# Declaring instructions on different banks of one PSUM pair free of each other

## The chip, the cores and the metric

The kernel runs on one core of a Trainium2 chip. A core has a matrix engine (TensorE, PE in the profile, its weight loads listed apart as PEld), three engines for element-wise work (VectorE, DVE; ScalarE, ACT; GpSimd, POOL) and queues that start transfers (DMA). Each engine works through its own list of instructions in the order in which they were written, and engines wait for each other through semaphores. The metric is the device time of one execution in microseconds (us).

PSUM is the memory into which PE writes. It has eight banks for each of its 128 partitions, each with 512 float32 values. This kernel uses all eight, as four pairs.

## The reference

Two layers follow each other. For 8 batches of 576 positions and 8 heads of width 64, the first is attention in a symmetric window of 32 positions. Its output, 512 numbers for a position, goes into the second: a router picks 2 of 4 experts for each position, each expert is a causal attention head of width 64 with an output projection, and the two picked outputs are added with the router's weights.

```python
scores = q @ k.T / 8                      # each batch and head
attn = softmax(where(abs(i - j) <= 32, scores, -1e9))
x = (attn @ v) as (batch, position, 512)
logits = x @ w_gate                       # (batch, position, 4)
w = softmax over the two largest logits
for e in range(4):
    a = softmax(causal((x @ wq[e]) @ (x @ wk[e]).T / 8))
    out += w[e] * (a @ (x @ wv[e]) @ wo[e])
```

## The kernel before

The whole work is cut into steps, and a text, `ORDER` (line 24), lists them in the order in which each engine is to meet them. There is no planner at run time: the loop at line 590 calls the function with the step's name, and the digits after the name are its arguments (batch, group of heads or pair of experts, tile). After `@` stand the PSUM banks that the step uses, and a letter names the engine of a copy: a for ACT, v for DVE, g for POOL. So `pt010@1` is the function `pt` for batch 0, expert pair 1, part 0, in bank 1, and `ot010@1a` is the copy of its result by ACT.

The steps of one batch, each with its engine:

- loads `lq`, `lk`, `lv` by the DMA queue of the sync engine. A load waits for the PE instruction that was written last before it (lines 175 to 179), so loads keep pace with PE;
- `tq`, `tk` (DVE) transpose q and k in blocks; `sc` (PE) makes the window's scores, `ex` (ACT) their exponentials, `mk` (POOL, at times DVE) the mask;
- `av` (PE) multiplies by v, `un` (DVE) divides by the sum, `xt` (PE) transposes the result, `xf` (ACT or DVE) copies it from PSUM, `xb` casts it to bfloat16;
- the gate: `ga` (PE) makes the logits, `gt` and `gm` (DVE, lines 442 to 456) transpose them and find the two largest, `ge` (ACT, line 448) takes exponentials, `gu` (DVE, lines 461 to 464) makes the weights. These five keep all that they need in one bank;
- the experts: `pp` and `pv` (PE) project, `pe` and `ve` copy the results out, `ps` (PE) makes scores, `xe` (ACT) exponentials, `se` (POOL) the causal mask, `po` (PE) multiplies by v, `oe` (DVE) divides and weighs, `pt` (PE) transposes, `ot` copies that out, `py` (PE) projects, `ye` copies to the tile Y, `st` stores.

Steps of several batches lie in each other's gaps in `ORDER`. All PE instructions are issued by `mm` (line 170) or `tr` (line 173), and all copies by `copy` (lines 152 to 158), so the profile shows these lines; which step it is follows from the tiles and the order.

What counts for this change is how PSUM is held. The four tiles `PS0` to `PS3` are pairs of banks:

```python
PS = [psum.tile([128, 2, 512], F32, name=f"PS{i}") for i in range(4)]
def two(bank):
    return PS[bank // 2]
def one(bank):
    return PS[bank // 2][:, bank % 2, :]
```

Banks 0 and 1 are `PS0`, 2 and 3 `PS1`, 4 and 5 `PS2`, 6 and 7 `PS3`. The wide steps (`sc`, `ex`, `av` and `un` of the first four tiles, `pp`, `pe`, `ps`, `xe`, `po`, `oe`) take a whole pair through `two`. The narrow ones take a single bank through `one`: the gate's five, `pt` and `ot`, and the last, shorter tile of `av`, `un`, `xt`, `xf`, `pv`, `ve`, `py` and `ye`. Two narrow steps can so stand in the two banks of one pair at the same time.

The framework in which the kernel is written draws the dependencies between instructions by itself, from the tiles that they write and read, and sets the waits on semaphores. In the kernel before, instructions of two engines on different banks of one pair do wait for each other in places: the trace shows PE on bank 1 released by DVE on bank 0.

Of the kernel before, what the change touches and what calls it, by code (L numbers as in the profile page):

```python
# [89 lines left out]
"""  # L90


@with_exitstack
def kernel(
    ctx: ExitStack,
# [8 lines left out]
    moe_wo: bass.AP,  # L104
    out: bass.AP,
):
    nc = tc.nc
    B, H, S_, D = q.shape
    E, DM, HD = moe_wq.shape
    assert S_ == S and D == 64 and H == 8 and HD == 64 and DM == 512 and E == 4  # L110
# [12 lines left out]
    PS = [psum.tile([128, 2, 512], F32, name=f"PS{i}") for i in range(4)]  # L123
# [19 lines left out]
    ident = sb.tile([128, 128], F32, name="ident")  # L143
# [51 lines left out]
        nc.scalar.activation(RC[1], RC[0], EXP)  # L195

    def s_ident():
        make_identity(nc, ident)
        nc.gpsimd.tensor_copy(ident_bf, ident)

    def s_ones():
# [386 lines left out]
    with tc.manual_schedule():  # L588
        nc.vector.memset(RC[0], 0.0)
        for step in ORDER.split():  # L590
            name, _, banks = step.partition("@")
# [35 lines left out]
```

The softmax here doesn't subtract the row's maximum and nothing guards it: scores larger than these inputs give would overflow.

## Time and profile before

| | |
|---|---|
| time, median of 3 runs | 263.46 us (263.01 to 265.67) |
| span of the profiled execution | 263.2 us |
| mean granted clock of PE | 0.978 |
| PE's share of the chain that ended last | 73% |
| DVE's, ACT's, DMA's share of it | 12%, 5%, 4% |
| read from and written to memory outside the core | 30.42 MB, 9.44 MB |

The chain that ended last is followed back from the last instruction: at each step to what released it, or to the instruction ahead of it on its engine. An engine's idle time matters only where this chain goes through it. In the timeline, a line is a run of like instructions: when it started, how long it took, engine, source line, operation, out<-in tiles, shape, count, and in brackets the idle time of the engine ahead of it with what ended it. A line "DVE L464" is the last instruction of `gu`, "PE L173 PS<-ident_bf,OE" is `pt`, "PE L170 PS<-WO,OTT" is `py`.

### The profile page before, as it was taken

Reading aid. Unit: us, or ns where it says so; the run is one execution under the profiler, and the core shown is the slowest. Engines: PE = TensorE matmul, PEld = TensorE weight load, DVE = VectorE, ACT = ScalarE, POOL = GpSimd, SP = SyncE. Lnnn points to the kernel's source line nnn. Section 1 sums busy time; section 2 is a strip of 40 time slices with the busy share of each in tenths; the row PEclk is TensorE's granted clock in tenths of the full one; section 3 lists DMA queues with packets and bytes.
Section 4 is the critical chain, followed back from the end, with each engine's and each line's share of the span. In section 5 each row is a group of like instructions: output and inputs, shape, how many; then the busy total and the mean of one; then the engine's idle time right before and its main releaser. Section 6 shows DMA issues by size and latency. Waiting matters only on the chain.

```text
span 263.2 us, 12340 instructions
## 1 busy us (share of the span) xinstructions
PE 217.3 (83%) x5523; PEld 173.8 (66%) x5536; DVE 186.4 (71%) x381; ACT 155.2 (59%) x236; POOL 149.0 (57%) x164
## 2 busy tenths in 40 slices
PE   0386988999997899889779699989799698998762
PEld 0375767877796588767567577867687476875440
DVE  7977868998889668768467778959655344467360
ACT  2057674886686476567626677637455675656333
POOL 5049778189949953489726932797535652311110
PEclk9999999999999799999999999999999799999798
DMA  7969578868888356598728533443302104040225
GB/s 244 283 174 268 120 158 269 224 192 208 215 243 212 122 139 204 165 241 214 244 65 232 170 112 95 125 133 75 110 22 85 72 11 182 2 158 5 101 93 189
DMA packets 55382, 40.65 MB, mean 154 GB/s; under 512 B 45345, under 2 KB 46369, under 8 KB 55329
## 3 DMA queue, kind: packets, MB, share of 16 engines
q1 hardware_dynamic: 54672, 38.62, 51.3%
q10 hardware_dynamic: 656, 1.25, 1.3%
q8 instruction: 43, 0.70, 1.0%
q14 instruction: 11, 0.08, 0.1%
HBM read 30.42 MB, written 9.44 MB: 151 GB/s over the span
## 4 chain that ended last, share of the span: by engine, by line
PE 73%; DVE 12%; issue 6%; ACT 5%; DMA 4%; SPq 0%; DVEq 0%; ACTq 0%
PE PS L170 65%; PE PS L173 8%; DVE XTB L158 2%; DMA kn<-in_k_dram 2%; DMA V<-in_v_dram 1%; ACT Y L154 1%; ACT A L346 1%; ACT ATE L516 1%; DVE Tkn L299 1%; DVE Tkn L287 1%; DVE Y L158 1%; DVE PS L442 1%; ACT OTT L154 1%; DVE OTT L158 1%; DVE XTF L158 0%
## 5 line engine op out<-in xcount | busy, mean ns | idle before, releaser
L350 POOL TENSOR_TENSOR A<-A,MASKP 128x576 f32<-128x576 f32 x62 | 87.2, 1428 | 43.2 <-ACT A L346 43.2
L516 ACT ACTIVATE ATE<-PS 128x1024 bf16<-128x1024 f32 (+1 forms) x64 | 51.0, 837 | 24.8 <-PE PS L170 23.5
L170 PE MATMUL PS<-Tqn,Tkn 32*64 32x128 f32 (+2 forms) x2560 | 46.4, 275 | 14.5 <-DVE Tqn L299 10.6
L346 ACT ACTIVATE A<-PS 128x576 f32<-128x576 f32 x64 | 38.6, 651 | 33.5 <-PE PS L170 30.4
L170 PEld LDWEIGHTS PS<-Tqn,Tkn 32*64 32x64 f32 x2560 | 40.9, 140 | 18.8 <-DVE Tqn L299 10.8
L523 POOL TENSOR_SCALAR_AFFINE_SELECT ATE<-ATE 128x512 bf16<-128x512 bf16 (+1 forms) x48 | 25.2, 539 | 42.9 <-ACT ATE L516 42.8
L170 PE MATMUL PS<-V,A 128*64 128x65 f32 (+1 forms) x1280 | 40.0, 222 | 7.3 <-issue 3.1
L170 PEld LDWEIGHTS PS<-V,A 128*64 128x64 f32 (+1 forms) x1280 | 36.3, 131 | 11.5 <-issue 4.8
L287 DVE STREAM_TRANSPOSE Tkn<-kn 128x576 f32<-128x576 f32 x28 | 32.6, 1242 | 3.2 <-PE PS L170 1.7
L287 DVE STREAM_TRANSPOSE Tqn<-qn 128x576 f32<-128x576 f32 x28 | 32.6, 1242 | 1.6 <-DMA qn<-in_q_dram 1.6
L170 PE MATMUL PS<-WO,OTT 128*128 128x512 bf16 (+1 forms) x83 | 19.6, 355 | 8.5 <-DVE G L464 2.5
L376 DVE TENSOR_TENSOR XN<-PS,RC 128x512 f32<-128x512 f32 x32 | 22.1, 692 | 1.2
L156 POOL COPY V<-V 64x1024 f32<-64x1024 f32 (+1 forms) x22 | 21.8, 993 | 1.8 <-POOL A L350 0.5
L154 ACT COPY XTF<-PS 128x1024 f32<-128x1024 f32 (+1 forms) x26 | 16.6, 676 | 8.0 <-PE PS L173 5.2
L170 PE MATMUL PS<-WV,XTB 128*128 128x256 bf16 (+1 forms) x192 | 20.0, 264 | 0.7 <-ACT ATE L516 0.4
L173 PE MATMUL PS<-ident,XN 128*128 128x128 f32 x144 | 19.7, 277 | 1.1 <-issue 0.8
L170 PE MATMUL PS<-XTB,WQ 128*128 128x288 bf16 x128 | 19.0, 296 | 1.5 <-DVE XTB L158 1.4
L154 ACT COPY Y<-PS 128x1024 f32<-128x1024 f32 (+1 forms) x18 | 15.0, 839 | 8.0 <-PE PS L170 7.4
L170 PE MATMUL PS<-XTB,WK 128*128 128x288 bf16 x128 | 19.6, 300 | 0.0
L156 POOL CAST XTB<-XTF 128x128 bf16<-128x128 f32 (+1 forms) x18 | 10.9, 622 | 13.3 <-ACT XTF L154 12.7
L170 PEld LDWEIGHTS <-ATE 128*128 128x128 bf16 x480 | 16.6, 97 | 2.5 <-issue 1.2
L173 PEld LDWEIGHTS PS<-ident,XN 128*128 128x128 f32 x144 | 15.6, 140 | 4.0 <-issue 2.7
(70 smaller groups left out, 271.8 us busy)
## 6 DMA issues: line engine op xcount, KB each, us to landing
V<-in_v_dram SPq DMA_DIRECT2D x32, 256.0 KB, 3.9
out_dram<-Y SPq DMA_DIRECT2D x16, 512.0 KB, 3.4
kn<-in_k_dram SPq DMA_DIRECT2D x14, 576.0 KB, 5.0
qn<-in_q_dram SPq DMA_DIRECT2D x14, 576.0 KB, 4.2
kn<-in_k_dram SPq DMA_DIRECT2D x4, 288.0 KB, 5.1
qn<-in_q_dram ACTq DMA_DIRECT2D x4, 288.0 KB, 5.5
V<-in_v_dram SPq DMA_DIRECT2D x8, 128.0 KB, 3.9
out_dram<-Y SPq DMA_DIRECT2D x15, 64.0 KB, 2.2
```

The source lines that it names most:

```text
L154: nc.scalar.copy(o, i)
L156: nc.gpsimd.tensor_copy(o, i)
L158: nc.vector.tensor_copy(o, i)
L170: PACE[0] = nc.tensor.matmul(*args, **kw)
L173: PACE[0] = nc.tensor.transpose(*args)
L287: nc.vector.transpose(T[:, dh, :].rearrange("q (p o) -> q o p", o=18), n_[:, :, 32 * dh:32 * dh + 32])
L299: nc.vector.transpose(QKT[nm][g][:, dh, :].rearrange("q (p o) -> q o p", o=18)[:, 9 * x:9 * x + 9, :], NAT[nm][g][:, 9 * x:9 * x + 9, 32 * ...
L346: nc.scalar.activation(a_part(b, g, half, p), two(b0)[:, :, 0:HS], EXP, scale=scale_att)
L350: (nc.gpsimd if eng == "g" else nc.vector).tensor_tensor(out=ap, in0=ap, in1=MASK[:, None, HS * half:HS * half + HS].to_broadcast([128, 2, ...
L376: nc.vector.tensor_tensor(out=XN[T // 2][:, T % 2, :].rearrange("p (g h d) -> p g h d", g=2, h=4), in0=u[:, :, :, 0:64], in1=rc[:, :, :, N ...
L516: nc.scalar.activation(A[:, at:at + 2 * step].rearrange("p (e x) -> p e x", e=2)[:, :, 0:w], two(b0)[:, :, 0:w], EXP, scale=scale_moe)
L523: nc.gpsimd.affine_select(ap, ap, pattern=[[0, n], [1, w]], compare_op=IS_GE, fill=0.0, base=64 * j if c == 3 else 0, channel_multiplier=-1)
```

## The change

The kernel's `nc` is wrapped. Each call on PE, DVE, ACT and POOL is issued as before, and then noted with the boxes that it reads and writes: tile, partitions and range; for a PSUM tile all partitions and whole banks. For each of the last 100 noted instructions of the same tile on another engine, if no two boxes overlap with at least one write, the wrapper declares that the two do not depend on each other. It is for the narrow steps above: two that stand in the two banks of one pair need not wait for each other any more. Instructions that start loads and stores are not noted. The step list, the instructions and their operands are the same.

```diff
--- before.py
+++ after.py
@@ -90,6 +90,62 @@
 """
 
 
+class Watched:
+
+
+
+    def __init__(self, tc):
+        self.tc, self.tiles = tc, {}
+        self.tensor, self.vector, self.scalar, self.gpsimd = (
+            Engine(self, e) for e in (tc.nc.tensor, tc.nc.vector, tc.nc.scalar, tc.nc.gpsimd))
+        self.sync = tc.nc.sync
+
+    @staticmethod
+    def boxes(i):
+        found = []
+        for aps, write in ((i.ins.ins, False), (i.ins.outs, True)):
+            for a in aps:
+                b = getattr(a, "bass_ap", None)
+                if b is None:
+                    continue
+                row, n = b.ap[0]
+                p0, lo = divmod(b.offset, row)
+                hi = lo + sum(st * (m - 1) for st, m in b.ap[1:]) + 1
+                if b.tensor.name.startswith("PS"):
+                    p0, n, lo, hi = 0, 128, 2 * lo // row, (2 * hi - 1) // row + 1
+                    row = 2
+                found.append((b.tensor.name, p0, p0 + n, lo / row, hi / row, write))
+        return found
+
+    @staticmethod
+    def clash(x, y):
+        return (x[0] == y[0] and (x[5] or y[5]) and x[1] < y[2] and y[1] < x[2] and x[3] < y[4] and y[3] < x[4])
+
+    def note(self, engine, i):
+        mine = self.boxes(i)
+        done = set()
+        for name in {x[0] for x in mine}:
+            seen = self.tiles.setdefault(name, [])
+            for e, theirs, j in seen:
+                if e is not engine and j.ins.name not in done:
+                    done.add(j.ins.name)
+                    if not any(self.clash(x, y) for x in mine for y in theirs):
+                        self.tc.declare_no_dep(i.ins, j.ins, reason="no common element")
+            self.tiles[name] = seen[-100:] + [(engine, mine, i)]
+        return i
+
+
+class Engine:
+    def __init__(self, watched, engine):
+        self._w, self._e = watched, engine
+
+    def __getattr__(self, name):
+        f = getattr(self._e, name)
+        if name == "dma_start":
+            return f
+        return lambda *a, **k: self._w.note(self._e, f(*a, **k))
+
+
 @with_exitstack
 def tile_sliding_window_symmetric__then__jetmoe_attn_experts_kernel(
     ctx: ExitStack,
@@ -104,7 +160,7 @@
     moe_wo: bass.AP,
     out: bass.AP,
 ):
-    nc = tc.nc
+    nc = Watched(tc)
     B, H, S_, D = q.shape
     E, DM, HD = moe_wq.shape
     assert S_ == S and D == 64 and H == 8 and HD == 64 and DM == 512 and E == 4
@@ -195,7 +251,7 @@
         nc.scalar.activation(RC[1], RC[0], EXP)
 
     def s_ident():
-        make_identity(nc, ident)
+        make_identity(tc.nc, ident)
         nc.gpsimd.tensor_copy(ident_bf, ident)
 
     def s_ones():
```

## Prediction

> **What bounds the kernel now.** I read the page first (its busy times, its clock row and the chain of waits that ended last), then the chain in order of time, then the timeline around each place where TensorE (PE) stood still, then windows over those places.
>
> ```profile
> span 263.2 us, 12340 instructions
> PE 217.3 (83%) x5523; PEld 173.8 (66%) x5536; DVE 186.4 (71%) x381; ACT 155.2 (59%) x236; POOL 149.0 (57%) x164
> PEclk9999999999999799999999999999999799999798
> PE 73%; DVE 12%; issue 6%; ACT 5%; DMA 4%; SPq 0%; DVEq 0%; ACTq 0%
> ```
>
> PE is busy for 83% of the span and is 73% of the chain; the rest of the chain is short visits to VectorE (DVE, 12%) and ScalarE (ACT, 5%). So the kernel is PE's work plus the stalls in PE's queue. Three digits of the clock row fall to 7, in slices of 6.6 us that begin near 86, 204 and 243 us (the 8 at the end is the tail). By windows, 0 to 84 us has 67.0 us of PE work and DMA engines busy for 0.80 of the time; 84 us to the end has 150.3 us of PE work in 179.2, so 28.9 us of PE idle, and DMA at 0.41. The question is how much of these 28.9 us is a wait between two banks of one pair. Three places in the timeline show the type:
>
> ```profile
> 84.14 0.10 PEld L173 LDWEIGHTS <-OE 128*128 128x128 bf16 x1
> 85.41 0.38 DVE L442 STREAM_TRANSPOSE PS<-PS 128x160 f32<-128x160 f32 x1
> 86.28 0.44 PE L173 MATMUL PS<-ident_bf,OE 128*128 128x128 bf16 x5 [2.07 <-DVE PS L445]
> ...
> 203.48 0.37 DVE L442 STREAM_TRANSPOSE PS<-PS 128x160 f32<-128x160 f32 x1 [2.08 <-PE PS L173]
> 205.18 1.02 PE L170 MATMUL PS<-WO,OTT 128*128 128x512 bf16 x3 [1.81 <-ACT A L346]
> 206.33 0.69 ACT L154 COPY OTT<-PS 128x640 bf16<-128x640 bf16 x1 [0.68 <-DVE G L464]
> 207.08 0.69 PE L173 MATMUL PS<-ident_bf,OE 128*128 128x128 bf16 x5 [0.88 <-ACT OTT L154]
> ...
> 245.00 0.64 PE L170 MATMUL PS<-WO,OTT 128*64 128x256 bf16 x4 [2.45 <-DVE G L464]
> ```
>
> The first is step pt010@1: five transposes into bank 1. They waited 2.07 us for the gate step gt2@0, which works in bank 0 of the same pair and which DVE could start only at 85.41, after other work. The third is py52@7, which waited 2.45 us for gate step gu7@6. Neither pair of steps shares an element: OE and OTT come from elsewhere, and the banks differ.
>
> ```profile
> 84.17:87.58 3.41, 1.34 (x17) 1.17 (x15) 2.09 (x6) 1.88 (x3) 3.35 (x4) 1.00 0.52 181
> 87.58:90.99 3.41, 3.19 (x12) 1.68 (x12) 2.90 (x10) 1.45 (x3) 3.41 (x4) 0.50 0.57 172
> 203.63:207.04 3.41, 0.97 (x3) 0.38 (x4) 2.04 (x11) 1.97 (x5) 1.83 (x2) 1.00 0.00 0
> 207.04:210.46 3.42, 3.38 (x18) 2.33 (x18) 0.67 (x1) 2.04 (x3) 2.29 (x2) 0.50 0.32 126
> 241.17:244.59 3.42, 1.38 (x33) 0.71 (x22) 2.21 (x11) 2.46 (x4) 1.47 (x3) 1.00 0.01 2
> 244.59:248.00 3.41, 3.00 (x16) 1.94 (x17) 0.32 (x2) 1.30 (x2) 0.64 (x1) 0.50 0.11 28
> ```
>
> These are windows over those places; after the length comes PE's busy time, and the number after the last bracket is the granted clock. Each time PE was busy for less than 1.4 us of 3.41, the next 3.41 us ran at half clock. So these stalls are paid twice.
>
> **What the Trainium skill says.** "PSUM — Partial Sum Buffer", section "PSUM bank collisions raise a hardware error", says that two engines on one bank and quadrant at once are an error, reads included, while the same pairs on different banks run clean. So a wait between two banks guards nothing; no trace here shows a collision. "TensorE: Matmul & The Clock Gate", section "What's actually happening", says that the clock is halved after an idle window of about 3.4 us of a free-running grid. The trace agrees on 3.41 us and on the half, but shows that a window with 0.97 to 1.38 us of work is idle enough. "Perfetto Trace Analysis", section "Identifying Dependency Chains", says that an instruction that waits for several engines may have extra wait instructions put ahead of it; PE's queue has 44 such semaphore instructions here, most of 0.05 us.
>
> **The change part by part.** No instruction is added or taken away and the step list is the same, so the busy times stay. The wrapper, whose host-side code costs the chip nothing, withdraws the dependency between two instructions of different engines unless they share a box: for PSUM a bank, for SBUF a range, with at least one write. Loads are not wrapped, so they keep their waits and their pacing. Pairs of reads of one bank (ACT and DVE) are freed too; PE refills the bank between them and both sides still wait for PE, so I put that at nothing. What is left is the sum over steps that sit alone in one bank of a pair. I list PE's idle time there from the timeline, and what I take after asking which true wait comes next.
>
> - pt010@1 behind gt2@0, 84.1: 2.07. The eight WQ matmuls behind it follow with no wait of their own. Take 2.0.
> - av34@3 behind ye02@2a, 106.0: 0.46. Take 0.45.
> - xf32@2a on ACT behind ot100@3v on DVE, 114.62. PE's gate matmuls truly wait for it, idle 0.84; ACT could have begun at 114.2 when PE's transposes ended. Take 0.4.
> - pt110@3 behind gu3@2, 119.4: 0.43 on the weight load, but the short matmul before overlaps. Take 0.3. py12@7 behind un44@6, 127.1: 0.27. Take 0.2.
> - pt200@1 behind gu4@0, 147.1: 2.75. Its successor pv30 needs the ACT step that ended at 144.7 and started at 147.35. Take 2.6.
> - ga5@1 behind ot300@0v, 175.2: 1.03. Take 1.0. Then gt5@1 on DVE waited for pt310@0 until 177.45, and behind it ACT's exponentials, for which PE idled 0.36 at 179.5. Take 0.3.
> - ve51@4a on ACT behind un64@5 on DVE: ACT starts at 186.85 in place of about 186.1, behind it the exponential for which PE idled 1.40 at 188.5. Take 0.7.
> - xt62@3 behind ye32@2v, 192.5: 0.26. Take 0.25.
> - gt6@6 on DVE behind pt410@7 on PE, 203.48: DVE idle 2.08. Behind gt6 ACT's ge6 waits, and behind ge6 the exponential for which PE idled 1.81. Then ot410@7a waited for gu6@6, and pt400@6 for ot410: another 0.88. Together 2.69. pt400@6 shares bank 6 with gu6, so that wait stays, but gu6 ends about 2 us sooner. Take 2.6.
> - av74@1 behind ot500@0a, 221.1: 1.15. Take 1.1.
> - py52@7 behind gu7@6, 245.0: 2.45. Take 2.4.
> - In the tail, ot711@3a on ACT behind ye62@2v on DVE: ACT runs at 255.14, though PE's transposes ended near 253.5; PE idles 1.61 for it. Take 1.4.
>
> The sum is 15.7 us. Halved clock: 3.41 us at half speed lose 1.7 us of work, three times: 5.1. The ceiling is 20.8 us.
>
> Two things take some back. Between these places ACT and DVE release PE's banks with little to spare (PE idles of 0.2 to 0.4 us for them are all along the timeline), so part of a freed microsecond meets the next true wait. And the clock's windows lie on a fixed grid, so another thin stretch (the tail, or the 2.35 us at 130 us in which PE waited for nothing that the profile shows, and which I leave as it is) may now fill one. The trace bounds neither; from 0 to all, I keep 70% of the stalls (11.0) and two of three half-clock spells (3.4): 14.4 us, so 263.46 - 14.4 = 249.1 us.
>
> **The rivals.**
> - Nearly all of it comes back: 263.5 - 20.8 = 242.7. For it: after 84 us DVE is busy for 113.9 of 179.2 us, ACT 103.8, POOL 93.2, so each has room to run earlier with PE. Against it: POOL is busy for 9.85 us of the 10 from 80 to 90.
> - The waits change their name. PE is released early and stops at the next ACT or DVE release. Half of the four large places (2.0, 2.6, 2.6, 2.4), none of the small ones and no clock: 4.8, so 258.7. For it: ACT and DVE hold 17% of the chain.
> - No change: DVE's and ACT's own queues set the pace, and only the tail's 1.4 remains: about 262. Against it: DVE and ACT were idle at these places or had work that nobody needed soon.
> - Slower. A wait that stood for several is gone, and the others appear on their own: some 30 more wait instructions in PE's queue at 0.05 make 1.5. Loads are paced by PE's progress, so a PE that runs ahead sends them into DMA engines already busy (0.62 to 0.66 from 90 to 152 us), and one late k load of 5.0 us to landing lies on the path in full: 263.5 + 1.5 + 5.0 - 3 (a fifth of the stalls) = 267. Against it: the only large DVE waits for loads are 1.6 and 1.5 us in the whole span.
>
> **How the numbers follow.** Main case 0.62, nearly all 0.12, renamed waits 0.14, no change 0.08, slower 0.04. So faster by over 1% (below 260.8) is 0.88, within 1% 0.08, slower 0.04. The range from 241.5 to 258.5 holds the main case with both ends of the take-back and the full case, and leaves out about half of the renamed case, the unchanged and the slower one.
>
> **What the profile after would show.** Right: the idle of 2.07, 2.75, 2.69 and 2.45 us at these steps gone, PE's busy time down by the clock share (about 3 of 217) and its share of the span up to 86% or more, DVE's and ACT's busy times unchanged, the digits 7 before the tail mostly gone. Wrong: equally long idle of PE in the same stretches under another releaser (ACT A, ACT ATE or DVE XTB), new half-clock windows elsewhere, or DVE waits for loads of several microseconds.

## The result, and the profile after

The changed kernel takes 241.92 us (median of 4 executions, 240.37 to 243.94). The kernel before, run beside it, took 263.47 us. The ratio is 0.9171, with a 95% interval from 0.9079 to 0.9264; here and below, a ratio leaves out the executions of a kernel that took over 1.5% longer than its fastest. The forecast was 249.1 us with a range from 241.5 to 258.5: right in direction and inside the range, but at its lower end. What happened is the rival "nearly all of it comes back" (242.7 us), which had been given a chance of 0.12.

The first lines of the page of the changed kernel, then its clock row, and the shares of the chain of waits that ended last:

```profile
span 241.0 us, 12278 instructions
PE 212.3 (88%) x5523; PEld 172.5 (72%) x5536; DVE 186.3 (77%) x381; ACT 154.6 (64%) x236; POOL 149.1 (62%) x164
PEclk9997699999999999999999999999999999999999
PE 74%; DVE 10%; DMA 7%; issue 3%; ACT 2%; SPq 0%; ACTq 0%; DVEq 0%
```

The page splits the gain by itself. Span less PE's busy time is PE's idle time: 263.2 - 217.3 = 45.9 us before and 241.0 - 212.3 = 28.7 after, so 17.2 us less idle. PE's busy time fell by 5.0 us with the same 5523 recorded matmuls, and 17.2 + 5.0 = 22.2 us is the whole difference of the two spans. Most of the 5.0 is the clock that the matmuls ran at: the three half-clock windows of the kernel before are worth 4.5 (last row of the table below), and the first 84 us, in which the changed kernel has a half-clock spell of its own, take 0.9 back. The other 1.4 come in small steps at places where waits went. DVE, ACT and POOL are busy as long as before, within 0.6 us. In the clock row the digits below 9 that stood near 86, 204 and 243 us are gone, and there is a new pair near 24 us, outside the stretch that the change was expected to touch. All wrapped instructions now carry line L146, that of the wrapper.

The window from 84 us to the end, with the columns as in the prediction (length, then PE, weight loads, DVE, ACT, POOL, granted clock, DMA share, GB/s):

```profile
84.00:241.00 157.00, 145.80 (x3548) 116.50 (x3557) 113.29 (x243) 104.35 (x158) 93.62 (x104) 1.00 0.48 146
```

PE is idle for 11.2 of these 157.0 us, where it was idle for 28.9 of 179.2. The timeline of the changed kernel at the three places that the prediction showed:

```profile
85.25 0.38 DVE L146 STREAM_TRANSPOSE PS<-PS 128x160 f32<-128x160 f32 x1
85.94 0.45 PE L146 MATMUL PS<-ident_bf,OE 128*128 128x128 bf16 x5
86.22 1.14 PE L146 MATMUL PS<-XTB,WQ 128*128 128x288 bf16 x8
...
190.03 0.35 DVE L146 STREAM_TRANSPOSE PS<-PS 128x160 f32<-128x160 f32 x1
191.65 0.44 PE L146 MATMUL PS<-ident_bf,OE 128*128 128x128 bf16 x5
191.92 1.03 PE L146 MATMUL PS<-WO,OTT 128*128 128x512 bf16 x3
...
224.51 0.36 DVE L146 STREAM_TRANSPOSE PS<-PS 128x160 f32<-128x160 f32 x1 [0.57 <-PE PS L146]
224.85 0.41 PE L146 MATMUL PS<-WO,OTT 128*64 128x256 bf16 x4
225.20 1.92 PE L146 MATMUL PS<-WV,XTB 128*128 128x256 bf16 x16
227.11 0.19 DVE L146 TENSOR_TENSOR G<-PS,su 128x20 f32<-128x20 f32 x1
```

No PE line here has a bracket, so PE did not stand idle before any of them. In the second group the gate's transpose (DVE at 190.03) starts before the transposes of PE that it used to follow (191.65). In the third, py52@7 runs at 224.85, and the gate step it used to wait for, gu7@6, ends only at 227.11 + 0.19: PE passed it by 2.4 us. The sixteen matmuls behind it take 1.92 us at full clock.

To see where each microsecond came back, I took the start of each of PE's 5536 weight loads in both traces; the shift between the two kernels (before less after) steps up where something was saved.

| place (time before, us) | forecast of the list | step in the shift |
|---|---|---|
| first 84 us of after: half clock at 21, waits on nothing shown at 81 and 85 us | 0 | -1.8 |
| pt010@1, 84 | 2.0 | +2.1 |
| 106, 115, 119, 127 | 0.45, 0.4, 0.3, 0.2 | +0.5, +0.9, +0.4, +0.4 |
| stall on nothing shown, 130 | 0 | +2.1 |
| pt200@1, 147 | 2.6 | +2.6 |
| ga5@1 and gt5@1, 175 to 179 | 1.3 | +1.6 |
| a k load that lands late | 0 | -1.1 |
| ve51@4a, 188; xt62@3, 192 | 0.7, 0.25 | +1.6, +0.3 |
| gt6@6 to pt400@6, 203 to 207 | 2.6 | +2.9 |
| av74@1, 221 | 1.1 | +1.2 |
| a wait on nothing shown, 226 | 0 | +0.9 |
| py52@7, 245 | 2.4 | +2.6 |
| tail, 255 | 1.4 | +1.7 |
| half clock at 88, 207, 245 | 5.1 | +4.5 |

These sum to 23.4; smaller lasting shifts, none over 0.5 us, give back 1.2 on balance, which makes the 22.2. The listed places gave 18.8 where the list had 15.7. Of the first row the half clock is 0.4 and the two waits 1.4; PE so came late to pt010@1, and part of that row and of the second one cancel. Between the places the shift stays level: behind pt200@1 it is 8.5 us, and 8.5 to 8.8 until 173. So what a place gave was not taken back by the next true wait.

### The profile page after: what moved, and what is told of

Same layout as the page of the kernel before. It is cut to its first block, busy times and chain, and to the rows that moved or that the text cites. A ratio compares the mean times of both kernels' runs of the same rounds, so it can differ in the third digit from the quotient of the medians.

```text
span 241.0 us, 12278 instructions
## 1 busy us (share of the span) xinstructions
PE 212.3 (88%) x5523; PEld 172.5 (72%) x5536; DVE 186.3 (77%) x381; ACT 154.6 (64%) x236; POOL 149.1 (62%) x164
## 4 chain that ended last, share of the span: by engine, by line
PE 74%; DVE 10%; DMA 7%; issue 3%; ACT 2%; SPq 0%; ACTq 0%; DVEq 0%
PE PS L146 74%; DMA kn<-in_k_dram 5%; DVE Tkn L146 3%; DVE Tqn L146 2%; DMA V<-in_v_dram 2%; DVE XTB L146 2%; DVE PS L146 1%; ACT V L146 1%; ACT Y L146 1%; ACT A L146 1%; DVE XTF L146 1%; ACT ATE L146 0%; DVE OTT L146 0%; SPq L350 0%; DVE m L146 0%
## 5 line engine op out<-in xcount | busy, mean ns | idle before, releaser
L146 POOL TENSOR_TENSOR A<-A,MASKP 128x576 f32<-128x576 f32 x62 | 87.5, 1435 | 35.7 <-ACT A L146 35.7
L146 ACT ACTIVATE ATE<-PS 128x1024 bf16<-128x1024 f32 (+1 forms) x64 | 51.0, 836 | 21.4 <-PE PS L146 19.0
L146 PE MATMUL PS<-Tqn,Tkn 32*64 32x128 f32 (+2 forms) x2560 | 46.2, 272 | 16.3 <-DVE Tqn L146 12.9
L146 ACT ACTIVATE A<-PS 128x576 f32<-128x576 f32 x64 | 38.5, 650 | 32.9 <-PE PS L146 27.7
L146 PEld LDWEIGHTS PS<-Tqn,Tkn 32*64 32x64 f32 x2560 | 40.4, 138 | 22.0 <-DVE Tqn L146 11.7
L146 POOL TENSOR_SCALAR_AFFINE_SELECT ATE<-ATE 128x512 bf16<-128x512 bf16 (+1 forms) x48 | 25.2, 539 | 28.9 <-ACT ATE L146 28.8
L146 PE MATMUL PS<-V,A 128*64 128x65 f32 (+1 forms) x1280 | 41.2, 227 | 1.8 <-issue 0.9
L146 PEld LDWEIGHTS PS<-V,A 128*64 128x64 f32 (+1 forms) x1280 | 37.6, 136 | 5.8 <-issue 3.4
L146 DVE STREAM_TRANSPOSE Tkn<-kn 128x576 f32<-128x576 f32 (+1 forms) x36 | 37.2, 1120 | 3.9 <-DMA kn<-in_k_dram 3.9
L146 DVE STREAM_TRANSPOSE Tqn<-qn 128x576 f32<-128x576 f32 (+1 forms) x36 | 37.3, 1118 | 1.3 <-DMA qn<-in_q_dram 1.3
L146 DVE TENSOR_TENSOR XN<-PS,RC 128x512 f32<-128x512 f32 (+1 forms) x40 | 25.5, 638 | 1.4
L146 POOL COPY V<-V 64x1024 f32<-64x1024 f32 (+1 forms) x22 | 21.5, 977 | 2.7 <-DMA V<-in_v_dram 1.1
L146 PE MATMUL PS<-WO,OTT 128*128 128x512 bf16 (+1 forms) x83 | 18.5, 341 | 2.6 <-ACT Y L146 1.1
L146 PE MATMUL PS<-ident,XN 128*128 128x128 f32 x144 | 19.5, 278 | 0.5 <-issue 0.5
L146 PE MATMUL PS<-XTB,WQ 128*128 128x288 bf16 x128 | 18.0, 286 | 2.0 <-DVE XTB L146 2.0
L146 ACT COPY XTF<-PS 128x1024 f32<-128x1024 f32 (+1 forms) x26 | 16.5, 674 | 5.0 <-PE PS L146 4.3
L146 PE MATMUL PS<-WV,XTB 128*128 128x256 bf16 (+1 forms) x192 | 18.7, 256 | 0.7 <-issue 0.6
L146 POOL CAST XTB<-XTF 128x128 bf16<-128x128 f32 (+1 forms) x18 | 11.4, 647 | 12.4 <-ACT XTF L146 11.8
L146 ACT COPY Y<-PS 128x1024 f32<-128x1024 f32 (+1 forms) x18 | 15.0, 840 | 5.9 <-PE PS L146 5.4
L146 PE MATMUL PS<-XTB,WK 128*128 128x288 bf16 x128 | 18.2, 286 | 0.0
L146 PEld LDWEIGHTS <-ATE 128*128 128x128 bf16 x480 | 16.6, 97 | 2.2 <-issue 0.9
L146 PE MATMUL PS<-VE,ATE 128*128 128x65 bf16 x480 | 17.6, 193 | 0.3 <-DVE VE L146 0.2
```

Of the source, the lines that this page charges most:

```text
L146: return lambda *a, **k: self._w.note(self._e, f(*a, **k))
```

## The experiments

Each experiment but the last three adds one rule to the wrapper: a pair is declared free only if the rule agrees too. The step's name is kept with each noted instruction. This is the common edit; the kernels differ in `free`.

```diff
             op = name.rstrip("0123456789")
+            nc.step = name
...
-                    if not any(self.clash(x, y) for x in mine for y in theirs):
+                    if not any(self.clash(x, y) for x in mine for y in theirs) and self.free(
+                            engine, self.step, mine, e, step, theirs):
```

The kernel before, run in the same jobs, took 265.05 us beside the gate, all-but-gate, PE-pair and ACT/DVE-pair kernels, 265.52 beside the read pairs and the three "keep" kernels, and 263.92 beside the last ones.

**Which steps: the gate, and all the rest.**

```diff
+    def free(self, e1, s1, b1, e2, s2, b2):                       # gate only
+        return any(s[:2] in ("gt", "gm", "ge", "gu") for s in (s1, s2))
...
+        return not any(s[:2] in ("gt", "gm", "ge", "gu") for s in (s1, s2))   # all but the gate
```

> Pairs are declared free only where one of the two belongs to a gate step gt, gm, ge or gu. Theory (PE's stalls behind the gate, and the half-clock windows that follow them, carry the gain): the large places at 84, 147, 203 and 245 us and the small ones at 119 and 178 come back, by the shifts seen after the full change 2.1 + 2.6 + 2.9 + 2.6 + 0.4 + 0.5 = 11.1 us, and the three half-clock windows 4.5 us: about 248 us. Rival (the gain is spread over all freed waits in proportion to their number): the gate is in under half of the freed pairs, so less than half of 21.5 us: 253 us or more.

> The complement: every pair is declared free except those in which one belongs to gt, gm, ge or gu. Theory: the small places away from the gate come back, 0.5 + 0.5 + 0.4 + 1.1 + 1.6 + 0.3 + 1.2 + 1.7 = 7.3 us, and the three half-clock windows after 84, 205 and 242 us stay: about 256 us. Rival (spread in proportion): 252 us or less. If the parts are additive, this gain and that of the gate's pairs add up to about 21.5 us.

Gate alone: 248.88 us, ratio 0.9423 (0.935 to 0.9496). All but the gate: 255.57 us, 0.9666 (0.9579 to 0.9754). Both times are as expected, though the second trace has its half-clock windows at 146 and 239 us and not where they were expected to stay. The two gains are 16.2 and 9.5 us; together 25.7, where the whole change gives about 23 on this base (265.05 to 242). They add up, within the widths of the intervals, so neither part runs into waits that the other removes. A take-back by true waits, which stay in all three kernels, would add up too. What speaks against it is the size: the list had 10.2 us of stalls at the gate's places, with the 5.1 of the clock 15.3 in full, and the gate alone gave 16.2.

**Which engines: pairs with PE, and pairs of ACT and DVE.**

```diff
+        return any(e is self.tc.nc.tensor for e in (e1, e2))          # pairs with PE
...
+        return not any(e is self.tc.nc.tensor for e in (e1, e2))      # pairs without PE
```

> Pairs are declared free only where one of the two is on PE; ScalarE and VectorE keep waiting for each other. Theory: all that is lost against the full change is what ScalarE held behind VectorE at 115, 187 and 255 us and the copy ot410 behind gu6, 0.5 + 0.7 + 1.6 + 0.5 = 3.3 us: about 245 us. Rival (the order between ScalarE and VectorE was the brake): half of the gain or more is missing, 252 us or more.

> Only pairs of ScalarE and VectorE (and GpSimd) are declared free, PE keeps all its waits. Theory: 0.4 + 0.7 + 1.4 = 2.5 us come back, the stalls of PE at 84, 147, 203 and 245 us and the three half-clock windows stay: about 261 us. Rival: 252 us or less.

Pairs with PE: 248.76 us, 0.9434 (0.9347 to 0.9522), which lies midway between the two theories. Pairs without PE: 258.98 us, 0.9782 (0.9687 to 0.9878), 2 us faster than expected. The gains are 16.3 and 6.1 us and sum to 22.4. So the change consists of these two parts, but the split was forecast wrongly: waits between ACT and DVE, which never stop PE directly, are worth more than 2.5 to 3.3 us. How much more is less sure: the interval of the ratio puts the 6.1 anywhere from 3.2 to 8.3 us. The timeline of ACT shows the place at 188 us. The first fence is the kernel before, the second the one that frees only pairs without PE:

```profile
186.85 0.54 ACT L154 CAST VE<-PS 64x128 bf16<-64x128 f32 x2 [2.28 <-DVE XN L382]
187.40 1.94 ACT L516 ACTIVATE ATE<-PS 128x1024 bf16<-128x1024 f32 x2
```

```profile
182.96 0.54 ACT L150 CAST VE<-PS 64x128 bf16<-64x128 f32 x2 [1.49 <-PE PS L150]
183.51 1.94 ACT L150 ACTIVATE ATE<-PS 128x1024 bf16<-128x1024 f32 x2
```

The releaser in the bracket changes from DVE's normalization (false) to PE's product in the same bank (true), and the wait shrinks from 2.28 to 1.49 us: 0.79, which is the step in this kernel's shift at 188 us (+0.79). With +0.7 at 207 us and +1.7 in the tail, such waits make 3.2 us of this trace. A further +2.4 is at 130 us, where a stall that no wait explains is absent; more on that below. The rest is half-clock windows that went and came.

The trace of the pairs with PE tells the same from the other side. Against the change it lacks 0.9 us at 115 us of the kernel before, 1.5 at 188, 0.8 behind py52@7 and 1.6 in the tail, together 4.8 (1.5 more is a half-clock window). The third place was not on the list. PE is early there, but ACT's copy of what py52@7 made in bank 7 still waits for gu7@6 in bank 6, and PE then waits for ACT's exponentials behind that copy, 0.74 us where the changed kernel has 0.21. So a false wait between ACT and DVE can come to light when the one on PE is gone:

```profile
231.37 0.37 ACT L150 COPY Y<-PS 128x256 f32<-128x256 f32 x1 [0.97 <-DVE G L150]
232.72 1.02 PE L150 MATMUL PS<-WO,OTT 128*128 128x512 bf16 x4 [0.74 <-ACT ATE L150]
```

**Which pairs: different banks, or two reads of one bank.**

```diff
+        return all(x[3] < y[4] and y[3] < x[4] for x in b1 for y in b2      # same-bank reads
+                   if x[0] == y[0] and x[0].startswith("PS"))
...
+        return not all(x[3] < y[4] and y[3] < x[4] for x in b1 for y in b2  # different banks
+                       if x[0] == y[0] and x[0].startswith("PS"))
```

> Only pairs that share a PSUM bank and both read it (and disjoint ranges in SBUF) are declared free; pairs on different banks keep their waits. Theory: both readers wait for PE's refill of the bank anyway, so nothing: 263.5 us. Rival (these are most of the waits between ScalarE and VectorE, 92 of 108): 4 us or more faster.

> Only pairs on different PSUM banks of one pair are declared free; two readers of one bank and disjoint ranges in SBUF keep their waits. Theory (the different banks carry the gain, the same-bank pairs nothing): as the full change, 242 us. Rival (the same-bank reads are worth the 1% that the run with them alone seemed to show): 244.5 us.

Same-bank reads (and disjoint ranges in SBUF) alone: a median of 264.85 us beside 265.52, ratio 0.99 (0.9854 to 0.9946). The ratio rests on only five of its 20 executions, which spread from 259.42 to 268.69 us; those of the kernel before spread from 262.61 to 269.72. The means of all are 264.35 and 266.02. The difference lies in the clock: the time lost to it, span times one minus the granted clock, is 6.8 us on average beside 9.3, and the time without it 257.5 beside 256.7. So no wait came back; why less was lost to the clock stays open. Different banks alone: 241.21 us, 0.9175 (0.9115 to 0.9236), against 0.9192 (0.914 to 0.9244) for the change in the same job. So the different banks carry the gain, and freeing the readers of one bank adds nothing to it. Fewer wait instructions are not the cause either: the pages count 12340 instructions before, 12300 with the reads alone and 12351 with the banks alone (those of one kernel differ by 13 between two traces).

The profiled execution of the read pairs is the shortest of the 20: its span is 257.7 us, 5.5 less than that of the kernel before, with all the large stalls in it. These are lines of its PE timeline, and below them windows over three of the thin stretches, each with the window that follows:

```profile
86.53 0.44 PE L151 MATMUL PS<-ident_bf,OE 128*128 128x128 bf16 x5 [1.66 <-DVE PS L151]
144.99 0.45 PE L151 MATMUL PS<-ident_bf,OE 128*128 128x128 bf16 x5 [2.75 <-DVE G L151]
202.66 1.02 PE L151 MATMUL PS<-WO,OTT 128*128 128x512 bf16 x4 [1.80 <-ACT A L151]
240.77 0.41 PE L151 MATMUL PS<-WO,OTT 128*64 128x256 bf16 x4 [2.44 <-DVE G L151]
```

```profile
140.55:143.96 3.41, 1.69 (x55) 0.84 (x39) 3.24 (x9) 2.07 (x4) 3.15 (x4) 1.00 0.85 236
143.96:147.38 3.42, 2.39 (x24) 2.15 (x25) 2.77 (x8) 1.02 (x3) 3.42 (x4) 1.00 0.82 248
201.98:205.40 3.42, 1.87 (x14) 1.13 (x14) 1.46 (x8) 2.75 (x6) 2.71 (x2) 1.00 0.00 0
205.40:208.81 3.41, 3.41 (x102) 2.58 (x101) 0.76 (x1) 2.96 (x5) 1.60 (x3) 1.00 0.40 154
239.53:242.94 3.41, 2.17 (x20) 1.63 (x20) 0.79 (x5) 1.47 (x3) 0.75 (x2) 1.00 0.04 11
242.94:246.36 3.42, 3.13 (x56) 2.00 (x56) 2.66 (x7) 2.10 (x3) 1.16 (x3) 1.00 0.53 186
```

The same stalls, and the clock stays at 1.00: here the borders of the grid cut each stall so that no window between 84 us and the tail has less than 1.6 us of work. In the shift of the weight loads, the steps where the three half-clock windows of the kernel before lay are 1.5, 1.8 and 1.3 us, 4.6 of the 5.5. So whether a stall also costs a half-clock window is a matter of where the grid lies in that execution, and one trace must not be read as if it showed the kernel's share of it.

**One stall put back at a time.** These are the change, with the waits between one PE step and one gate's steps kept.

```diff
+        gate = ("gt7", "gm7", "ge7", "gu7")
+        return not ("py52" in (s1, s2) and (s1 in gate or s2 in gate))
...
+        gate = ("gt4", "gm4", "ge4", "gu4")      # with "pt200"
...
+        gate = ("gt2", "gm2", "ge2", "gu2")      # with "pt010"
```

> The changed kernel with one wait put back: py52@7 (PE, bank 7) again waits for gate 7 (gt7, gm7, ge7, gu7 in bank 6). Theory: PE stands still for about 2.5 us again and the next clock window runs at half speed, 1.7 us more: 241.9 + 4.2 = 246.1 us. Rival (a stall costs its length alone): 244.4. Rival (the stall is absorbed since everything else is earlier): 242.

> The changed kernel with one other wait put back: pt200@1 again waits for gate 4 in bank 0. In the kernel before this stall of 2.75 us was followed by no half-clock window. Theory: PE stands still for 2.6 us again; whether a clock window is thin enough depends on where the grid lies, so 244.5 us without and 246.2 with a half-clock window, and the trace says which. Rival (absorbed): 242.

> The changed kernel with a third wait put back: pt010@1 again waits for gate 2 in bank 0, early in the span, with 150 us of work behind it. Theory: 2.1 us of stall and 1.7 us of half clock stay on the path to the end: 245.7 us. Rival (later slack takes an early stall back): 242 to 243.

With py52@7 held: 245.42 us (0.9257), 3.5 over the change. With pt200@1 held: 246.63 us (0.9299), 4.7 over it. With pt010@1 held: 243.68 us (0.9212), 1.8 over it. The change itself is taken at 241.92 here, from another job, so each of these differences is uncertain by about 2 us, and the third is not clear of nothing. The traces are sharper: against that of the change, the weight loads fall back at these places by 3.4, 4.2 and 1.2 us. Lines of the three timelines, in that order, one fence for each kernel, and then their windows:

```profile
226.85 0.64 PE L151 MATMUL PS<-WO,OTT 128*64 128x256 bf16 x4 [2.43 <-DVE G L151]
```

```profile
140.93 0.46 PE L151 MATMUL PS<-ident_bf,OE 128*128 128x128 bf16 x5 [2.75 <-DVE G L151]
```

```profile
86.15 0.44 PE L151 MATMUL PS<-ident_bf,OE 128*128 128x128 bf16 x5 [1.33 <-DVE PS L151]
```

```profile
223.20:226.60 3.40, 1.22 (x26) 0.56 (x18) 2.22 (x11) 2.31 (x4) 1.47 (x3) 1.00 0.00 0
226.60:230.00 3.40, 3.15 (x17) 2.02 (x18) 0.19 (x1) 1.30 (x2) 0.63 (x1) 0.50 0.14 36
```

```profile
137.80:141.20 3.40, 0.65 (x7) 0.28 (x6) 2.97 (x7) 2.94 (x5) 3.15 (x4) 1.00 0.90 235
141.20:144.60 3.40, 3.40 (x21) 2.42 (x19) 2.73 (x3) 0.00 (x0) 3.40 (x3) 0.51 0.39 147
```

```profile
82.70:86.10 3.40, 1.97 (x82) 1.41 (x83) 3.33 (x6) 2.21 (x3) 3.28 (x5) 1.00 0.82 271
86.10:89.50 3.40, 3.35 (x28) 2.44 (x28) 1.75 (x9) 2.10 (x5) 3.40 (x4) 1.00 0.44 123
```

The stalls of py52@7 (2.43 us) and pt200@1 (2.75) come back at their size of before, and both are followed by a window at 0.50. 2.4 + 1.7 = 4.1 and 2.75 + 1.7 = 4.5, beside 3.4 and 4.2 in the traces and 3.5 and 4.7 in the times. In the kernel before, the stall of pt200@1 had no half-clock window behind it, because the grid split it in two:

```profile
142.20:145.61 3.41, 2.11 (x83) 1.31 (x75) 3.18 (x10) 2.02 (x5) 3.15 (x4) 1.00 0.84 252
145.61:149.03 3.42, 1.92 (x20) 1.77 (x21) 2.77 (x7) 1.34 (x2) 3.42 (x3) 1.00 0.91 267
```

The third experiment missed what was expected of it. Its stall is 1.33 us and not 2.07, since PE came to pt010@1 later in that trace while the gate step started at nearly the same time; and with 1.97 us of work its window was not followed by half clock. Whether the stall stays on the path to the end is not shown: the span of this trace is 240.7 us, no longer than the 241.0 of the change. It does show that the -1.8 of the first row of the table and the +2.1 of the second belong together: a delay before 84 us shortens that stall.

**One load earlier.** The changed kernel has one new wait of size, on DVE for a k load:

```profile
170.90 2.34 DVE L146 STREAM_TRANSPOSE Tkn<-kn 128x576 f32<-128x576 f32 x2 [1.40 <-DMA kn<-in_k_dram]
```

The edit moves one word of `ORDER`; the lines are cut short, and the slash stands for the lines between the two places.

```diff
-    ... xf52@2a ye20@6v lv70 ...  /  ... lv73 lk71 po310@4 ...
+    ... xf52@2a lk71 ye20@6v lv70 ...  /  ... lv73 po310@4 ...
```

> The changed kernel with the k load lk71 placed nine steps of PE earlier in the list, some 6 us; nothing else. In the changed kernel VectorE idled 1.40 us for this load at 170.9 us, and PE 0.69 and 0.70 us at 173.6 and 176.6, after which 1.1 us of the shift against the kernel before was lost. Theory (stalls are paid in full now, none is taken back): that idle is gone in the trace and the time is about 1 us shorter, 241 us, less than a few runs can tell for sure. Rival (another wait ends next): PE's idle at these places stays.

> The changed kernel unchanged, for a second trace and more times beside the others: 242 us. What the trace tells: whether the stalls of 2 us and more stay gone at all places (theory: yes), whether PE again passes the place at 130 us of the kernel before without the stall that no wait explains, and how many half-clock windows there are between 84 us and the tail (none in the first trace; theory: 0 or 1, since no thin stretch is left).

In the trace with the load moved the wait is gone:

```profile
168.11 2.33 DVE L146 STREAM_TRANSPOSE Tkn<-kn 128x576 f32<-128x576 f32 x2
```

PE's weight loads gain 1.1 us at that place. But the trace with different banks alone, in which the load stands where it was, has no such wait either, and PE gains the same 1.1 us:

```profile
168.63 2.33 DVE L151 STREAM_TRANSPOSE Tkn<-kn 128x576 f32<-128x576 f32 x2
```

In the six traces of the change and its near kin with the load unmoved (the change twice, different banks, and the three with one stall put back) this wait is 1.40, 1.12, 0.56 and 0.23 us and twice nothing. It comes and goes from execution to execution, so one trace cannot show that moving the load ended it. The time is 241.22 us (0.9137, 0.9091 to 0.9183) beside 242.77 for the change run again (241.01 to 244.68, 0.9192). The medians differ by 1.5 us and the intervals overlap, so whether it beats the change stays open.

The second trace of the change has no stall of 2 us or more after 84 us and no half-clock window from there to the tail. Its longest waits are 1.45 us on nothing shown, at 101 us, and 1.14 in the tail.

**The kernel before, looked at again.**

> The kernel before unchanged, for a second trace. Theory: PE's stalls at 84, 147, 175, 203, 221, 245 and 255 us recur to within 0.3 us, since they follow from the list; the half-clock windows come after some of the thin stretches but not after the same ones, since their grid runs free of the kernel; the stall near 130 us that no wait explains recurs if it belongs to the program.

It took 264.59 us, with a profiled span of 262.9. These are lines of its PE timeline, then its clock row, then windows over the stall at 84 us and over another at 130 us:

```profile
85.97 0.44 PE L173 MATMUL PS<-ident_bf,OE 128*128 128x128 bf16 x5 [1.56 <-DVE PS L445]
130.77 2.22 PE L170 MATMUL PS<-V,A 128*64 128x65 f32 x49 [2.62 <-issue]
145.88 0.71 PE L173 MATMUL PS<-ident_bf,OE 128*128 128x128 bf16 x5 [2.75 <-DVE G L464]
205.04 1.02 PE L170 MATMUL PS<-WO,OTT 128*128 128x512 bf16 x4 [1.81 <-ACT A L346]
244.74 0.64 PE L170 MATMUL PS<-WO,OTT 128*64 128x256 bf16 x4 [2.45 <-DVE G L464]
```

```profile
PEclk9997999999999999999979799999999799999798
```

```profile
83.78:87.19 3.41, 1.85 (x54) 1.59 (x39) 2.09 (x6) 1.89 (x3) 3.32 (x4) 1.00 0.50 179
87.19:90.60 3.41, 3.41 (x58) 2.33 (x57) 2.91 (x10) 2.78 (x5) 3.41 (x4) 1.00 0.56 172
128.16:131.57 3.41, 0.80 (x27) 0.80 (x28) 0.59 (x1) 0.00 (x0) 0.31 (x1) 1.00 0.04 12
131.57:134.98 3.41, 3.41 (x109) 3.24 (x104) 2.74 (x5) 0.00 (x0) 0.00 (x0) 0.50 0.49 119
```

The stalls of 2.75, 1.81 and 2.45 us recur at the same length; the one at 84 us is 1.56 in place of 2.07, outside the 0.3 us that were expected. Of the half-clock windows, those at 207 and 244 us recur, the one at 88 us does not, and there are new ones at 131.6 and 145.2 us. The large stalls belong to the kernel; which of them a half-clock window follows differs from execution to execution.

## Why the prediction was right in its mechanism and short in its size

- **The stalls are false waits between banks, and they sit in PE's queue.** Right. Freeing different banks alone gives 0.9175, the same as the change. The four large stalls (2.07, 2.75, 2.69, 2.45 us) are gone and no wait of that length took their place, which refutes "the waits change their name" (258.7). The gate's pairs alone are worth 16.2 us, and two of the stalls, put back one at a time, come back with their half clock.
- **Reads of one bank at nothing.** Right as to the change: different banks alone are as fast. Freed by themselves, the reads give back no wait, though these executions lost less to the clock.
- **"I keep 70% of the stalls (11.0)."** This is the term that was too small. PE's idle time fell by 17.2 us, more than the whole list of 15.7; over all executions the time without the loss to the clock fell by 18.2 (256.7 to 238.5). The reason given for the 70% was that ACT and DVE release PE's banks "with little to spare", with idles of 0.2 to 0.4 us all along the timeline. The timeline doesn't bear this out: after 84 us PE waits for ACT or DVE eight times for 0.18 to 0.46 us, and four of these are false waits of the list. The changed kernel has five such waits. ACT and DVE wait for PE's products, and once PE is early they are early too, which fits the level shift between the places. The rival's argument, DVE busy for 114 of 179 us and so free to follow, was the right one, and it was read and given 0.12.
- **"Two of three half-clock spells (3.4)."** Near in size, but its ground was not right: the three places were read as fixed, and they vary from execution to execution. Every execution has its granted clock on record. Over 41 executions of the kernel before, the time lost to the clock is 8.8 us on average; over 10 of the changed kernel it is 4.1. So on average 4.8 us of the gain are the clock (an upper figure, since PE isn't busy all of that time), which fits that most windows thin enough to be followed by half clock are gone.
- **"The 2.35 us at 130 us ... which I leave as it is."** It went, with 2.1 us, so the total came this much nearer to the full case by something that the prediction had left out. It can't be credited to the change with certainty. A wait of this kind recurs there in the second trace of before (2.62) and, shorter, in three of the experiments (all but the gate 2.13, read pairs 1.80, pt010@1 held 1.40); in the others it is at most 1.05, and in the two traces of the changed kernel 0.45 and nothing. In before an instruction fetch of 16 KB lies at 130.17 to 131.13 us. That a fetch is its cause is argued and not shown; no run was made that moves the fetch alone.
- **Sizes in the list.** ve51@4a, where the false wait holds ACT, was put at 0.7 us and gave 1.6, of which 0.8 with the pairs of ACT and DVE alone. The next step after av74@1 (+0.9 at 226 us, of which 0.4 is given back at once) is a wait on nothing shown of 0.53 us in both traces of before that the changed kernel's doesn't have. The waits between ACT and DVE were 2.5 us on the list and 3.2 to 4.8 in the traces, with the copy behind py52@7 as a place that the list lacks.
- **The transfers.** The "slower" rival named a late k load of 5.0 us on the path. A late k load did come, in some executions: where it was longest it cost 1.1 us, not 5.0. The extra wait instructions that it also feared didn't: the page counts 62 instructions fewer.

Three things stay open: the cause of the stall at 130 us, why the kernel with the reads alone lost less to the clock, and whether the version with the earlier load is faster.

## What to carry to other kernels

A PSUM tile that holds two banks ties narrow steps together that share nothing. On a kernel bound by PE, look in the timeline for a PE step whose releaser works in another bank, ask which true wait comes next, and if the engines behind it have room, count the stall in full: a discount needs a wait in the profile that would really stay behind. Look for the same false waits between ACT and DVE too: they don't carry PE's name, and some show only when PE no longer waits itself. It was enough here to free instructions on different banks (241.21 us); two readers of one bank can keep their waits.

## What the runs showed of the hardware

The half clock comes in windows of 3.41 us on a grid whose place differs between the traces. I laid the grid over the fourteen traces by their clock steps and took every full-clock window from the first recorded step on, without the tail. All 25 windows with 0.66 to 1.49 us of PE work were followed by half clock. Of 50 windows with 1.52 to 2.17 us two were (1.70 and 1.71), and of 825 with more none. So on this kernel a window in which PE is busy for up to 44% can still bring half clock on, and each half-clock window costs up to 1.7 us of PE work. The Trainium skill, "TensorE: Matmul & The Clock Gate", section "What's actually happening", ties half clock to an idle window of a free-running grid. Its half and its 3.41 us agree with the traces; its word idle doesn't quite.

Ten of the fourteen traces have a half-clock spell that begins between 21 and 24 us. In eight it lasts two windows, the second of them behind a window with 1.9 to 3.1 us of PE time, itself at half clock; why, the runs don't show. The ends of matmuls are modelled in the trace, so the border between 1.49 and 1.52 us is not as sharp as it looks.
